# Where a second-layer operand is staged between two matrix products of a one-core kernel: out of the buffers of the weight jobs, into the places of the streamed weights

## The chip, the cores and the metric

The kernel runs on one core of a Trainium2 chip. The metric is the device time of one execution in microseconds. The engines are named as the profile names them: PE (TensorE, matrix products), DVE (VectorE), ACT (ScalarE), POOL (GpSimd), SP (SyncE, which only issues DMAs). Each engine runs its own instructions in order; DMAs are issued from the queues of SP, ACT and POOL.

## The reference

```
x  = attention(q, k, v)              # 8 x 8 heads, 576 x 64, masked with decay gamma^(i-j)
x  = x.reshape(4608, 512)
h  = (x @ w1) * (x @ w2)             # 512 -> 1024
x2 = (h @ w3) @ w_out                # 1024 -> 512; w3 @ w_out is multiplied out once
h2 = x2 @ w_in                       # 512 -> 2048
g  = h2 * clip(h2 + 3, 0, 6) / 6
out = g @ w_out2                     # 2048 -> 512, float32
```

## The kernel before

Every float32 operand is split into a high part (rounded on ACT) and a low part (a subtraction on DVE, `sub`, L134), and a product is three matmuls: high by high, high by low, low by high. The program is written as a sequence of ticks: one tick is three matmuls of 512 columns (`mm3`, L129 to L131, or seven matmuls per four ticks in the seven-product part), and `at(s, f)` puts f's instructions into the program at tick s. A tick sets only an order: each engine runs ahead of it or behind it as its waits allow. SP above all runs far ahead.

**Blocks.** After a prologue that multiplies w3 by w_out into W (high part `Wh`, low part `Wl`, `Wm`), the first layer runs over nine blocks j = 0 to 8 of 512 tokens. A block begins with `ffn1`: 16 products pa and pb (8 values f, for w1 and w2) in 64 ticks, four PSUM banks in turn. ACT copies pa out (`a_copy`, L642), DVE multiplies by pb (`s_mul`, L670 to L674), ACT rounds (`s_hi`, L681), DVE subtracts (`s_lo`, L134 with `pair`). Block 0 and block 8 have an older form (`ab_mul`, L657, `ab_hi`, L661). Between the products stand four "excursions" per block, the attention of a later block in small matmuls (L213); behind each, DVE has `v_scale` (L203), `z_sum` (L281), `p_mask` (L227), `s_add` (L246), `x_out` (L290) and `x_lo` (L134), ACT has `z_copy` (L274) and `x_hi` (L298).

**Seven products.** In blocks 1 to 7 the product of h with W is made of seven half-size products instead of eight (`px_str`, L769, 32 ticks). Its weights are sums of quarters of W, kept in the DRAM scratch `wsd` and streamed 1 MB at a time by SP (`load_w`, L726) into three places: two halves of the tile `wb`, and a third in the x tile of the block that has just been used (`w3`, tag `xl`). Product i + 3 is loaded into the place of product i. The first two loads of the next block are issued as soon as their places are free.

**x2.** The result of a block is x2, in the x tile with tag `xh` (`rt`). It is prepared for the second layer in two halves m = 0 and 1: four sums (`x2_sums`, DVE), high part (`x2_hi`, L812, ACT), low part (`x2_lo`, DVE), and two stores of 896 KB in 1 KB pieces to `xod` (`x2_store`, L822, from ACT's queue). This stands at ticks 1, 2, 3 and 7 behind the block for m = 0, and 14 ticks later for m = 1, so in the next block's ffn1. Sums and low part go to `stg`, the high part to `stg_hi`.

**Jobs.** `stg` and `stg_hi` also carry the weights of the second layer: per block a job i (w_in) and a job q (w_out2). A job loads two raw pieces on SP (`fetch`, L106), unpacks them into `stg` (`weights`: ACT L154, L155; DVE L159, L163) at ticks s to s + 5, has four sums (L838) at s + 10, the high part (ACT, L841) at s + 11, the low part at s + 14 and two stores (L849, ACT's queue) at s + 19. Job i stands at s = 30 of the block, job q at 58; in the last block at 24 and 50.

**The last block.** W is read back from `wsd` into the place of `wb` (`w_again`, L577 to L582, ten DMAs, 4 MB) from tick 2 of block 8 on. The first operands of the second layer (`load_xop`, L902, 1 MB each) come from tick 24 on. In block 0, `w_quads` (L565 to L570, ten DMAs, 4 MB) stores W's quarters at tick 20, and four `w_job`s make the other weights of the stream at ticks 65, 73, 81 and 97.

Of the kernel before, what the change touches and what calls it, by code (L numbers as in the profile page):

```python
# [26 lines left out]
def retention_moe_kernel(  # L27
# [57 lines left out]
    wsd = dram_p.tile([8, 128, 2, 4, 256], F32, name="wsd")  # L85
# [233 lines left out]
    with tc.manual_schedule():  # L319
# [152 lines left out]
        for t in range(2 * TPB, NTI):  # L472
            ex[t] = B0 + SPB * (t // TPB - 1) + 16 + 22 * (t % TPB)
# [83 lines left out]
        def open_sw():  # L557
            st["wb"] = Wp.tile([128, 2, 2, 4, 256], F32R, tag="Wh", name="wb")
# [50 lines left out]
        at(B0 + 20, w_quads)  # L609
        for q, d in enumerate((65, 73, 81, 97)):  # L610
# [5 lines left out]
        def ffn1(j):  # L616
# [29 lines left out]
            def f_b(f):  # L646
# [41 lines left out]
                for d, f_ in enumerate((s_mul, s_hi, s_lo) if j in STR else (ab_mul, ab_hi, ab_lo)):  # L688
# [664 lines left out]
```

## Time and profile before

| | us |
|---|---|
| time, median of 3 runs | 1558.53 (1558.18 to 1559.66) |
| the profiled execution | 1558.04 |
| its span, first to last instruction | 1556.2 |
| PE busy | 1453.1 (93% of the span) |
| DVE busy | 1111.3 (71%) |
| ACT busy | 587.1 (38%) |
| POOL busy | 139.9 (9%) |
| mean granted clock of PE | 0.979 of full speed |

An engine is busy while one of its instructions runs; issuing a DMA and waiting are not counted. The blocks j = 0 to 8 lie from 72.75 to 855.03 us of the span, the second layer from there to the end. A wait is read from the idle time ahead of an instruction, shown in brackets with what ended it. A granted clock below 1.00 in a stretch means that PE ran part of it at 1.2 instead of 2.4 GHz.

### The profile page before, as it was taken

The page shows a single profiled execution, that of the slowest core. Times are in us where ns is not written, and L with a number is a line of the kernel's source. Part 1 is how long each engine was busy: PE and PEld are TensorE (multiplying, and loading weights), DVE is VectorE, ACT ScalarE, POOL GpSimd, SP SyncE. Part 2 cuts the span into 40 slices and gives each one's busy share as a digit, 9 for nine tenths or more (in the row PEclk, how much of TensorE's full clock was granted, in tenths as well). Part 3 has the DMA queues.
Part 4 walks back from the last instruction along what each step waited for, and adds up shares of the span by engine and source line. Part 5 has one row for each costly group of instructions (what it writes and reads, how often), then busy time and mean ns, then how long its engine had stood idle before and what let it go on. Part 6 is the DMA issues. An engine that isn't in the chain of part 4 may idle for free.

```text
span 1556.2 us, 27873 instructions
## 1 busy us (share of the span) xinstructions
PE 1453.1 (93%) x11315; PEld 1219.0 (78%) x11315; DVE 1111.3 (71%) x1916; ACT 587.1 (38%) x878; POOL 139.9 (9%) x293
## 2 busy tenths in 40 slices
PE   9998898988988898887959999999999999999999
PEld 4577687776867777776848789888888888888888
DVE  7878576757568585767723766566667988888887
ACT  7563242323334242423412434333334434444443
POOL 1000000000000000000000124222222000000000
PEclk9999999999999999999989999999999999999999
DMA  9774667674857666684687987464688644444442
GB/s 353 264 243 149 231 231 264 236 282 174 317 173 271 220 239 255 213 293 165 236 323 300 337 305 257 177 242 169 259 312 315 192 136 136 136 137 136 133 140 75
DMA packets 195056, 351.30 MB, mean 226 GB/s; under 512 B 10384, under 2 KB 143280, under 8 KB 185072
## 3 DMA queue, kind: packets, MB, share of 16 engines
q1 hardware_dynamic: 122832, 212.88, 39.4%
q0 software_dynamic: 21792, 73.72, 12.8%
q10 hardware_dynamic: 50304, 62.92, 11.9%
q8 instruction: 89, 1.46, 0.4%
q14 instruction: 39, 0.32, 0.1%
HBM read 231.51 MB, written 117.96 MB: 225 GB/s over the span
## 4 chain that ended last, share of the span: by engine, by line
PE 52%; DMA 18%; DVE 17%; ACT 8%; issue 3%; SPq 1%; ACTq 0%; POOL 0%; DVEq 0%; POOLq 0%
PE pb L1275 15%; DMA xod<-stg 9%; DMA wqd<-stg 8%; PE pb L1276 8%; PE pb L129 8%; PE pb L131 8%; PE pb L130 8%; DVE stg L134 3%; PE Wps L512 3%; DVE x L290 2%; DVE stg L159 1%; ACT stg L154 1%; DVE stg L163 1%; ACT sign L155 1%; ACT pair L681 1%
## 5 line engine op out<-in xcount | busy, mean ns | idle before, releaser
L1275 PE MATMUL pb<-wq,op 128*128 128x512 f32 x1000 | 346.7, 391 | 0.0
L1276 PE MATMUL pb<-wq,op 128*128 128x256 f32 x1000 | 280.0, 280 | 0.0
L1275 PEld LDWEIGHTS pb<-wq,op 128*128 128x128 f32 x1000 | 187.0, 187 | 41.0
L129 PE MATMUL pb<-xop,wset 128*128 128x512 f32 (+1 forms) x558 | 205.6, 369 | 2.0 <-DMA xop<-xod 1.4
L130 PE MATMUL pb<-xop,wset 128*128 128x512 f32 (+1 forms) x558 | 205.2, 368 | 0.0
L131 PE MATMUL pb<-xop,wset 128*128 128x512 f32 (+1 forms) x558 | 205.2, 368 | 0.0
L1153 ACT CAST op<-unit 128x1024 fp32r<-128x1024 f32 x126 | 131.6, 1052 | 173.6 <-DVE unit L1139 152.8
L1276 PEld LDWEIGHTS pb<-wq,op 128*128 128x128 f32 x1000 | 189.0, 189 | 0.0
L134 DVE TENSOR_TENSOR op<-unit,op 128x1024 fp32r<-128x1024 f32 x126 | 153.9, 1222 | 30.6 <-ACT op L1153 30.6
L769 PE MATMUL px<-pair,wb 128*128 128x256 f32 x1176 | 154.3, 291 | 15.0 <-ACT pair L681 5.7
L769 PEld LDWEIGHTS px<-pair,wb 128*128 128x128 f32 x1176 | 148.2, 197 | 20.5 <-ACT pair L681 7.3
L129 PE MATMUL pb<-xh,w2h 128*128 128x512 f32 x288 | 120.2, 417 | 35.3 <-DVE sraw L674 12.8
L129 PE MATMUL pa<-xh,w1h 128*128 128x512 f32 x280 | 113.7, 406 | 28.0 <-ACT a L642 26.9
L129 PEld LDWEIGHTS pb<-xop,wset 128*128 128x128 f32 x558 | 105.2, 189 | 20.4 <-issue 1.8
L131 PEld LDWEIGHTS pb<-xop,wset 128*128 128x128 f32 x558 | 105.2, 189 | 17.5
L130 PEld LDWEIGHTS pb<-xop,wset 128*128 128x128 f32 x558 | 105.2, 189 | 17.3
L130 PE MATMUL pb<-xl,w2h 128*128 128x512 f32 x288 | 117.0, 406 | 0.0
L131 PE MATMUL pb<-xh,w2l 128*128 128x512 f32 x288 | 116.9, 406 | 0.0
L130 PE MATMUL pa<-xl,w1h 128*128 128x512 f32 x280 | 112.1, 400 | 0.2 <-DVE xl L134 0.2
L131 PE MATMUL pa<-xh,w1l 128*128 128x512 f32 x280 | 111.5, 398 | 0.0
L134 DVE TENSOR_TENSOR stg<-x 128x256 f32<-128x256 f32 x31 | 13.1, 422 | 125.7 <-DMA wqd<-stg 64.7
L129 PEld LDWEIGHTS pb<-xh,w2h 128*128 128x128 f32 x288 | 56.7, 197 | 53.5 <-issue 14.8
(200 smaller groups left out, 2330.1 us busy)
## 6 DMA issues: line engine op xcount, KB each, us to landing
wb<-wsd SPq DMA_DIRECT2D x49, 1024.0 KB, 5.7
unit<-gd SPq DMA_DIRECT2D x72, 512.0 KB, 5.3
xop<-xod SPq DMA_DIRECT2D x28, 1024.0 KB, 6.7
qk<-in_qk_dram POOLq DMA_DIRECT2D x36, 512.0 KB, 6.7
kv<-in_kv_dram POOLq DMA_DIRECT2D x32, 512.0 KB, 5.7
gd<-gw POOLq DMA_DIRECT2D x60, 256.0 KB, 2.9
gd<-g POOLq DMA_DIRECT2D x57, 256.0 KB, 3.8
xod<-stghi ACTq DMA_DIRECT2D x16, 896.0 KB, 4.7
```

The source lines that it names most:

```text
L129: nc.tensor.matmul(out=out_ap, lhsT=sh, rhs=mh, start=first, stop=False, **kw)
L130: nc.tensor.matmul(out=out_ap, lhsT=sh, rhs=ml, start=False, stop=False, **kw)
L131: nc.tensor.matmul(out=out_ap, lhsT=sl, rhs=mh, start=False, stop=last, **kw)
L134: eng.tensor_tensor(out=out_ap, in0=x, in1=y, op=ALU.subtract)
L154: nc.scalar.activation(out=c["u"], in_=high, func=ACTF.Abs, scale=2.0 ** -112)
L155: nc.scalar.activation(out=c["s"].bitcast(F16).rearrange("p (n t) -> p n t", t=2)[:, :, 1], in_=high, func=ACTF.Copy, scale=2.0 ** -64)
L290: nc.vector.scalar_tensor_tensor(out=c["x32"][:, p, a:a + n], in0=c["z"][:, p, a:a + n], scalar=cw[:, m, p:p + 1], in1=ut[:, p, 0:n], op0= ...
L512: nc.tensor.matmul(out=ps, lhsT=w3f[:, n // 4 % 8, n % 4 * 128:n % 4 * 128 + 128], rhs=wo[:, j, :], start=j == 0, stop=j == KF - 1)
L769: nc.tensor.matmul(out=out_ap, lhsT=w[:, x, kk, ms], rhs=y, start=k not in seen, stop=kk == 3 and x == 1, skip_group_check=True)
L1153: nc.scalar.copy(out=op_tiles(7 * b + p)[0], in_=src())
L1275: nc.tensor.matmul(out=c[k], lhsT=h[:, ts], rhs=w, start=first and kt == 0, stop=False, skip_group_check=True)
L1276: nc.tensor.matmul(out=c[k][:, 0:256], lhsT=l[:, ts], rhs=w[:, 0:256], start=False, stop=kt == 7, skip_group_check=True)
```

## The change

Six things change:

- x2 of blocks 1 to 7 no longer goes through `stg` and `stg_hi`. Its sums go to a new tile `xs` (the other x tile of the block, tag `xl`, which held the third streamed weight), one half of it for each m; its high and low parts go to the two halves of `wb`, the same for both m. Stores stand at tick 6 instead of 7, and m = 1 stands 16 ticks behind m = 0 instead of 14.
- `wsd` is laid out so that a streamed weight is read in pieces of 2 KB instead of 8 KB.
- `w_again` moves from tick 2 to tick 30 of block 8, and the memset of the sign tile (`late_sign`) from 0 to 23.
- `w_quads` moves from tick 20 to 44 of block 0, the last `w_job` from 97 to 104.
- Job i moves from tick 30 to 22, job q from 58 to 50 (in the last block from 50 to 48).
- The excursions of a block stand at 19, 40, 61 and 82 instead of 16, 38, 60 and 82, and `s_lo` one tick later.

```diff
-    wsd = dram_p.tile([8, 128, 2, 4, 256], F32, name="wsd")
+    wsd = dram_p.tile([8, 4, 128, 2, 256], F32, name="wsd")
...
-            ex[t] = B0 + SPB * (t // TPB - 1) + 16 + 22 * (t % TPB)
+            ex[t] = B0 + SPB * (t // TPB - 1) + 19 + 21 * (t % TPB)
...
-            st["wb"] = Wp.tile([128, 2, 2, 4, 256], F32R, tag="Wh", name="wb")
+            st["wb"] = Wp.tile([128, 2, 4, 2, 256], F32R, tag="Wh", name="wb")
...
-        at(B0 + 20, w_quads)
-        for q, d in enumerate((65, 73, 81, 97)):
+        at(B0 + 44, w_quads)
+        for q, d in enumerate((65, 73, 81, 104)):
...
-                for d, f_ in enumerate((s_mul, s_hi, s_lo) if j in STR else (ab_mul, ab_hi, ab_lo)):
+                for d, f_ in zip((0, 1, 3), (s_mul, s_hi, s_lo)) if j in STR else enumerate((ab_mul, ab_hi, ab_lo)):
...
-            nc.sync.dma_start(out=t.rearrange("p h k n -> p (h k n)").bitcast(F32), in_=wsd[WORD[i]].rearrange("p h k n -> p (h k n)"))
+            nc.sync.dma_start(out=t.rearrange("p k h n -> p k (h n)").bitcast(F32), in_=wsd[WORD[i]].rearrange("k p h n -> p k (h n)"))
...
-            for m, s in enumerate((now[0], now[0] + 14)):
-                def start(m=m):
-                    raw2.update({0: rt[:, m], 1: rt[:, 2 + m]})
-                    x2b["hi"], x2b["lo"] = stg_hi, stg
-                    x2_sums()
-
-                for d, f in ((1, start), (2, x2_hi), (3, x2_lo), (7, lambda m=m: x2_store(j, m))):
-                    at(s + d, f)
+            xs = x_ps[e].tile([128, 2, 4, 256], F32, tag="xl", name="xs")
+            hl = [st["wb"][:, i].rearrange("p k h n -> p (k h) n") for i in range(2)]
+            for m, s in enumerate((now[0], now[0] + 16)):
+                b1, b2, d = rt[:, m], rt[:, 2 + m], xs[:, m]
...
+                def sums(d=d, v=(b11, b12, b21, b22)):
+                    for o, a, b in ((0, v[1], v[0]), (1, v[3], d[:, 0]), (2, v[3], v[1]), (3, v[2], d[:, 1])):
+                        sub(nc.vector, d[:, o], a, b)
+
+                def hi(parts_=parts_):
+                    for a, b, t in parts_:
+                        nc.scalar.copy(out=hl[0][:, a:b], in_=t)
+
+                def lo(parts_=parts_):
+                    for a, b, t in parts_:
+                        sub(nc.vector, hl[1][:, a:b], t, hl[0][:, a:b])
+
+                def store(m=m):
...
+                    for h, t in enumerate(hl):
+                        nc.scalar.dma_start(out=xod[sb][:, :, m, h, a:a + HB1].rearrange("o p n -> p o n"), in_=t[:, 0:7].bitcast(F32))
+
+                for x, f in ((1, sums), (2, hi), (3, lo), (6, store)):
+                    at(s + x, f)
...
-            job(("i", n), (w_in2[n + NSET], w_in2[n]), A_SUMS, lambda hl, n=n: wid[n, hl], B0 + SPB * n + SPB + (30 if n < NSET - 1 else 24))
+            job(("i", n), (w_in2[n + NSET], w_in2[n]), A_SUMS, lambda hl, n=n: wid[n, hl], B0 + SPB * n + SPB + (22 if n < NSET - 1 else 24))
...
-                lambda hl, n=n: wqd[:, :, n, hl].rearrange("o p n -> p o n"), B0 + SPB * n + SPB + (58 if n < NSET - 1 else 50))
+                lambda hl, n=n: wqd[:, :, n, hl].rearrange("o p n -> p o n"), B0 + SPB * n + SPB + (50 if n < NSET - 1 else 48))
...
...
-        at(E0, late_sign)
+        at(E0 + 23, late_sign)
-        for i, s in enumerate((24, 52, 26, 28, 32, 38, 104)):
+        for i, s in enumerate((24, 58, 26, 28, 32, 38, 104)):
...
-        at(B0 + SPB * (STR[-1] + 1) + 2, w_again)
+        at(B0 + SPB * (STR[-1] + 1) + 30, w_again)
```

The first place in which the order of instructions matters is DVE at the start of a block (here block 6): the last sum of the seven products, then x2 of m = 0. Before, everything is written to `stg`, which a job's store may still be reading:

```order
L744 TENSOR_TENSOR x_5635<-x_5635,px 128x2x256 x2
L134 TENSOR_TENSOR stg<-x_5635 128x256
L134 TENSOR_TENSOR stg<-x_5635,stg 128x256
L134 TENSOR_TENSOR stg<-x_5635 128x256
L134 TENSOR_TENSOR stg<-x_5635,stg 128x256
L134 TENSOR_TENSOR stg<-x_5635,stghi 128x512
L134 TENSOR_TENSOR stg<-x_5635,stghi 128x256
L134 TENSOR_TENSOR stg<-stg,stghi 128x1024
```

The same instructions of DVE in the changed kernel, at the same place:

```order
L746 TENSOR_TENSOR x_5643<-x_5643,px 128x2x256 x2
L134 TENSOR_TENSOR xs<-x_5643 128x256
L134 TENSOR_TENSOR xs<-x_5643,xs 128x256
L134 TENSOR_TENSOR xs<-x_5643 128x256
L134 TENSOR_TENSOR xs<-x_5643,xs 128x256
L134 TENSOR_TENSOR wb<-x_5643,wb 128x512
L134 TENSOR_TENSOR wb<-x_5643,wb 128x256
L134 TENSOR_TENSOR wb<-xs,wb 128x1024
```

Their number and their sizes are the same; what they write to is another place.

The second place is DVE at the end of ffn1 (block 5), where the seven products are about to begin: `zp`, `P`, `S`, `x` and `xl` are an excursion's work, `stg` a job's, `keep` and `sraw` the `s_mul` of f = 7, and `pair` its `s_lo`, on which the third product waits. Before:

```order
L134 TENSOR_TENSOR xl<-x_5611,xh 128x4x128
L159 SCALAR_TENSOR_TENSOR stg<-stg,sign 128x512
L163 SCALAR_TENSOR_TENSOR stg<-wr,stg 128x512
L673 TENSOR_TENSOR keep<-a,pb 128x256
L674 TENSOR_TENSOR sraw<-a,pb 128x256
L134 TENSOR_TENSOR sraw<-keep,sraw 128x256 x2
L134 TENSOR_TENSOR keep<-sraw 128x256
L134 TENSOR_TENSOR pair<-sraw,pair 128x768
L838 TENSOR_TENSOR stg<-stg 128x256 x4
L134 TENSOR_TENSOR stg<-stg,stghi 128x1792
```

DVE at the same place of the changed kernel:

```order
L859 TENSOR_TENSOR stg<-stg 128x256 x4
L281 TENSOR_TENSOR zp<-zp,z 128x512
L227 TENSOR_TENSOR P<-sc,mask 128x512
L244 COPY S<-sc 128x256
L246 TENSOR_TENSOR S<-S,sc 128x256
L290 SCALAR_TENSOR_TENSOR x_5627<-zp,cw,ut 128x128 x4
L134 TENSOR_TENSOR xl<-x_5627,xh 128x4x128
L134 TENSOR_TENSOR stg<-stg,stghi 128x1792
L675 TENSOR_TENSOR keep<-a,pb 128x256
L676 TENSOR_TENSOR sraw<-a,pb 128x256
L134 TENSOR_TENSOR sraw<-keep,sraw 128x256 x2
L134 TENSOR_TENSOR keep<-sraw 128x256
```

The job's four sums and its 1792-column subtraction have moved from behind the last `pair` row to ahead of it, and the last unpacking (L159, L163) out of this stretch. The `pair` row is the next one.

The third place is SP in block 8: the end of `w_again` (`Wh`, `Wl`, `Wm`), the raw pieces of the last jobs (`wr`) and the operands of the second layer (`xop`). Before:

```order
L582 DMA Wl<-wsd 128x4x256
L577 DMA Wh<-wsd 128x4x256
L579 DMA Wl<-wsd 128x256
L580 DMA Wm<-wsd 128x3x256
L106 DMA wr<-in_w_in_dram 128x512 x2
L902 DMA xop<-xod_66 128x2048 x4
L106 DMA wr<-in_w_out_dram 128x512
```

SP in the changed kernel, from the same DMA of `w_again` on:

```order
L584 DMA Wl<-wsd 128x4x256
L579 DMA Wh<-wsd 128x4x256
L581 DMA Wl<-wsd 128x256
L582 DMA Wm<-wsd 128x3x256
L923 DMA xop<-xod_66 128x2048
L106 DMA wr<-in_w_out_dram 128x512
L923 DMA xop<-xod_66 128x2048
L106 DMA wr<-in_w_out_dram 128x512
```

The raw pieces of job i and three of the `xop` loads now stand ahead of `w_again`, and the raw pieces of job q right behind it.

## Rows read from the trace of the kernel before

**Rows 1.** Windows, span and busy: blocks 2 to 7; ffn1; seven products; block 8

```profile
core 0: us, PE busy (x) PEld busy (x) DVE busy (x) ACT busy (x) POOL busy (x), PEclk, DMA share, GB/s
244.94:771.01 526.07, 462.88 (x4994) 394.33 (x4993) 353.24 (x704) 176.65 (x276) 28.56 (x45) 0.96 0.66 236
331.06:391.90 60.84, 52.97 (x546) 42.51 (x545) 37.88 (x75) 19.88 (x32) 3.82 (x6) 0.97 0.58 204
655.88:681.46 25.58, 23.10 (x281) 22.18 (x280) 21.05 (x45) 8.95 (x14) 1.27 (x2) 1.00 0.89 322
771.01:833.27 62.26, 46.43 (x194) 37.54 (x193) 25.20 (x41) 17.39 (x28) 0.59 (x8) 0.89 0.77 276
```

**Rows 2.** Waits of PE, blocks 2 to 7: us in total, times, longest

```profile
PE pa L129 <- ACT a L642: 13.7, 6, 3.1
PE pb L129 <- DVE sraw L674: 12.8, 5, 4.1
PE sc L213 <- DVE kv L203: 12.1, 12, 1.8
```

**Rows 3.** Waits of DVE, blocks 2 to 7, in the same columns

```profile
DVE stg L134 <- DMA wqd<-stg: 49.9, 6, 9.0
DVE stg L134 <- DMA xod<-stg: 38.5, 6, 8.4
```

**Rows 4.** Timeline of DVE, block 3: start, duration, instruction, [idle before]

```profile
340.07 0.43 DVE L134 TENSOR_TENSOR stg<-x 128x256 f32<-128x256 f32 x1 [8.12 <-DMA wqd<-stg]
...
388.29 0.68 DVE L670 TENSOR_TENSOR sraw<-a,pb 128x512 f32<-128x512 f32 x1
...
397.50 0.69 DVE L159 SCALAR_TENSOR_TENSOR stg<-stg,sign 128x512 int32<-128x512 int32 x1 [0.58 <-ACT sign L155]
...
401.15 0.96 DVE L134 TENSOR_TENSOR pair<-sraw,pair 128x768 fp32r<-128x768 f32 x1 [0.56 <-ACT pair L681]
402.03 1.55 DVE L838 TENSOR_TENSOR stg<-stg 128x256 f32<-128x256 f32 x4
405.33 2.03 DVE L134 TENSOR_TENSOR stg<-stg,stghi 128x1792 fp32r<-128x1792 f32 x1 [1.75 <-ACT stghi L841]
```

**Rows 5.** Timeline of PE, the seven products of block 3

```profile
401.17 0.38 PE L769 MATMUL px<-pair,wb 128*128 128x256 f32 x1 [1.20 <-ACT pair L681]
402.16 5.22 PE L769 MATMUL px<-pair,wb 128*128 128x256 f32 x29 [0.61 <-DVE pair L134]
```

**Rows 6.** DMA from 392 to 403, weights alone: packets, MB, share; issues

```profile
q1 hardware_dynamic: 432, 3.15, 77.0%
...
wb<-wsd SPq DMA_DIRECT2D x3, 1024.0 KB, 4.8
```

**Rows 7.** DMA from 360 to 368, stores of x2 alone

```profile
q10 hardware_dynamic: 1824, 1.84, 69.3%
...
xod<-stg ACTq DMA_DIRECT2D x1, 896.0 KB, 6.3
```

**Rows 8.** DMA issues from 403 to 430, all three queues: KB, us to landing

```profile
wb<-wsd SPq DMA_DIRECT2D x4, 1024.0 KB, 8.4
...
wqd<-stg ACTq DMA_DIRECT2D x1, 896.0 KB, 20.6
```

**Rows 9.** Timeline of PE, block 0

```profile
109.50 0.77 PE L129 MATMUL pb<-xh,w2h 128*128 128x512 f32 x1 [3.50 <-DVE ab L657]
...
129.74 0.57 PE L213 MATMUL sc<-kv 64*64 64x64 f32 x15 [4.62 <-DVE kv L203]
```

**Rows 10.** Timeline of ACT, block 0

```profile
105.98 0.66 ACT L154 ACTIVATE stg<-wr 128x512 f32<-128x512 f32 x1 [9.91 <-DMA wr<-in_w_dram]
```

**Rows 11.** Timeline of ACT, block 8

```profile
811.03 0.66 ACT L154 ACTIVATE stg<-wr 128x512 f32<-128x512 f32 x1 [16.75 <-DMA xod<-stg]
```

**Rows 12.** Timeline of PE, block 8

```profile
814.53 0.80 PE L129 MATMUL pa<-xh,w1h 128*128 128x512 f32 x1 [13.23 <-ACT a L642]
```

**Rows 13.** DMA from 88 to 105: 1 KB stores of W

```profile
DMA packets 4663, 5.69 MB, mean 335 GB/s; under 512 B 203, under 2 KB 4299, under 8 KB 4661
```

More of the change, by code (lines that the diff above doesn't have):

```diff
@@ L576, in w_again @@
             for o, (c, k) in enumerate(quads):
-                nc.sync.dma_start(out=h[:, k:k + 4, c:c + 256].bitcast(F32), in_=wsd[o, :, 0])
+                src = wsd[o].rearrange("k p h n -> p h k n")
+                nc.sync.dma_start(out=h[:, k:k + 4, c:c + 256].bitcast(F32), in_=src[:, 0])
                 if k:
-                    nc.sync.dma_start(out=lo[0][:, 4:5, c:c + 256].bitcast(F32), in_=wsd[o, :, 1, 0:1])
-                    nc.sync.dma_start(out=lo[1][:, :, c:c + 256].bitcast(F32), in_=wsd[o, :, 1, 1:4])
+                    nc.sync.dma_start(out=lo[0][:, 4:5, c:c + 256].bitcast(F32), in_=src[:, 1, 0:1])
+                    nc.sync.dma_start(out=lo[1][:, :, c:c + 256].bitcast(F32), in_=src[:, 1, 1:4])
                 else:
-                    nc.sync.dma_start(out=lo[0][:, 0:4, c:c + 256].bitcast(F32), in_=wsd[o, :, 1])
+                    nc.sync.dma_start(out=lo[0][:, 0:4, c:c + 256].bitcast(F32), in_=src[:, 1])
         def w_job(q, s):
@@ L603, in store @@
                 for hl, t in enumerate((st["w"][1], st["w"][0])):
-                    nc.scalar.dma_start(out=wsd[4:8, :, hl, q].rearrange("o p n -> p o n"), in_=t[:, 1].rearrange("p (o n) -> p o n", o=4))
+                    nc.scalar.dma_start(out=wsd[4:8, q, :, hl].rearrange("o p n -> p o n"), in_=t[:, 1].rearrange("p (o n) -> p o n", o=4))
             for d, f in ((0, sums), (2, hi), (3, lo), (6, store)):
                 at(s + d, f)
-        at(B0 + 20, w_quads)
-        for q, d in enumerate((65, 73, 81, 97)):
+        at(B0 + 44, w_quads)
+        for q, d in enumerate((65, 73, 81, 104)):
             w_job(q, B0 + d)
@@ L730, in px_str @@
             rt = x_ps[e].tile([128, 4, BLK1], F32, tag="xh", name="x1")
-            st["w3"] = x_ps[e].tile([128, 2, 4, 256], F32R, tag="xl", name="wb")
+            st["w3"] = x_ps[e].tile([128, 4, 2, 256], F32R, tag="xl", name="wb")
             a, c, b, d = turn
@@ L768, in px_str @@
                         for x, y in ((0, hi), (0, lo), (1, hi)):
-                            nc.tensor.matmul(out=out_ap, lhsT=w[:, x, kk, ms], rhs=y, start=k not in seen, stop=kk == 3 and x == 1, skip_group_check=True)
+                            nc.tensor.matmul(out=out_ap, lhsT=w[:, kk, x, ms], rhs=y, start=k not in seen, stop=kk == 3 and x == 1, skip_group_check=True)
                             seen.add(k)
```

13 lines of the change are left out of this document (9 added, 4 removed).

## The prediction

> **What bounds the kernel now.** I read the windows first. Blocks 2 to 7 take 526.07 us, 87.7 each; PE is busy for 462.88 of them, so it stands idle for 63.2 us (10.5 a block), and the granted clock is 0.96, which is 4% of 87.7 = 3.5 us a block lost to stretches at 1.2 GHz [rows 1]. Nothing else is near full: DVE is busy for 353.24 us, 58.9 a block. So PE bounds these blocks, with holes, and the question is who makes the holes. PE's own waits name DVE and ACT: 13.7 us for `a_copy`, 12.8 for the `s_mul` of a large f, 12.1 for `v_scale` [rows 2]. DVE's waits say why it was late: 49.9 us for the store of job q and 38.5 for x2's own store of m = 0, together 88.4 us or 14.7 a block, all ahead of x2's sums [rows 3]. Block 3 shows the pattern: the sums of m = 0 wait 8.12 us at 340.07, because job q's low part still leaves `stg` [rows 4]. That store takes 20.6 us from issue to landing, where a store of the same size takes 6.3 behind its twin with nothing else in flight [rows 7, 8]. DVE takes its instructions in order, so `s_mul` and `v_scale` stand behind the blocked sums, PSUM banks stay full, and PE stops. Behind a stop the clock drops.
>
> **x2 out of `stg`.** No instruction is added. Before, x2's sums waited for job q and for x2's first store, and job i's unpacking for x2's second store. Now the sums write `xs`, which no DMA reads, so both waits of DVE [rows 3] lose their reason. What replaces them: the high and low parts of m = 1 go to the same halves of `wb` as those of m = 0 and must wait for the stores of m = 0. These are issued at tick 6, m = 1's high part stands at tick 18. Twelve ticks are 12 x 0.68 = 8.2 us, where a tick is 51.2 us of ffn1 without its three excursions (7.7 us), divided by 64. A store alone lands in 6.3 us [rows 7], and the queue is then empty of job q, which is issued 8 ticks earlier. I take no wait here; if the stores land as late as 10 us, 2 us a block. Behind the waiting instruction ACT has `s_hi` and `z_copy`, and PE has 12 ticks before it misses a bank, so even that is mostly covered.
>
> What is late next is DVE's own queue. Without the blocked 14.7 us it has 58.9 us of work a block plus its pauses for ACT, against PE's 74.3 (below). In ffn1 the load is dense, and the end of ffn1 gets more: ahead of the last `pair` row there now stand job q's sums and low part. Before, from the `s_mul` of f = 3 (388.29) to the end of `s_hi` of f = 7 (401.1) was 12.8 us [rows 4]. Out go two unpackings of 2 x 0.69 with their 0.6 us waits for ACT, 3.9 us. In come the sums 1.55, ACT's high part that now stands ahead of `z_copy` and costs DVE 1.75, and the low part 2.03 [rows 4]: 5.3 us. So 14.2 us. PE needed that row at 401.17 - 1.20 = 399.97 [rows 5]. If DVE starts the stretch as late as before, PE waits 1.2 + 1.4 = 2.6 and then 0.6 for `s_lo`, 3.2 us; if it is 2 us later, because PE itself no longer waits for it in ffn1, 5.2. I take 4.3, against 1.8 before. `s_lo` one tick later lets other work into DVE's pauses for `s_hi`, such as the 0.56 us at 401.15 [rows 4]; I count nothing for it.
>
> **A block now.** PE alone: ffn1 52.97 us busy at clock 0.97, less 3% of 60.84, is 51.1; the seven products at clock 1.00 are 23.10 [rows 1]; 74.2. To this come 4.3 for the pair, 0.9 for `v_scale` (2.0 before, 12.1 / 6; the half that came from blocked DVE goes), 0.5 for a weight that is late, and 1.7 for the clock (half of 3.5, one drop behind the pair wait). Sum 81.6, against 87.7: 6.1 us a block, 36.6 over the six. As a check, 74.2 + 10.5 + 3.5 = 88.2 gives the block before within 0.5.
>
> **2 KB pieces.** A load of 8 KB pieces moves 3.15 MB in 77.0% of 16 engines x 11 us, 23.2 GB/s per engine; stores in 1 KB pieces 1.84 MB in 69.3% of 16 x 8 us, 20.7 [rows 6, 7]. 2 KB lies between, so a 1 MB load occupies its engines for 2.8 to 3.2 us, at most 0.3 more, and lands after some 5 us alone. The gap that matters is contention: with all queues busy a load takes 8.4 us and a 1 KB store 20.6 [rows 8], as if the queues took turns by piece. Then smaller pieces shorten the store and lengthen the load. The slack of a load is two products, 6 us, plus the pair wait; job q's stores are issued 8 ticks earlier and overlap loads that are wanted later. I keep 0.5 us a block, with 0 and 3 as ends. The Trainium skill, DMA: Bandwidth & Descriptors, section Queues, rings and completion order, says that each DMA engine takes turns between its queues by packet; the two latencies above agree in direction. By it a load of 32 pieces per engine gives way to at most 32 pieces of 1 KB, which at 20.7 GB/s are 1.6 us; that lies between the ends above.
>
> **The first two loads of a block** now wait for x2's second store, since their places hold x2. Job q's raw pieces stand behind them on SP, and ACT and DVE wait for those. By ticks: m = 1's stores leave at about 21 us of the block (DVE some 4 us behind tick 22), land at 27, both loads at 33, the raw pieces at 35; job q wants them at tick 50, 39 us. Cost nothing; that cover is 4 us thick.
>
> **Blocks 0 and 1.** `w_quads` moved behind the last raw pieces on SP. Before, ACT waited 9.91 us for a raw piece queued behind those ten DMAs [rows 10]; DVE went idle, and PE lost 3.50 and then 4.62 us to its backlog [rows 9]. SP runs ahead of ticks, so `w_quads` really moves by some 5 us only, which is enough. Gain 8, between 3 and 10. Job 0 now comes 8 ticks earlier, onto a store of block 0 that still uses `stg`: +1 (0 to 3). Together -7.
>
> **Block 8.** PE waited 13.23 us for `a_copy`, behind ACT's 16.75 for x2's store [rows 11, 12]. That goes. But `w_again` (4.2 MB) now starts when x2's last store has landed, and job q's raw pieces stand behind it on SP. From tick 22 (15 us) to the second raw piece move: x2's stores 1.8 MB, four `xop` 4.2, `w_again` 4.2, job i's stores 1.8, a fifth `xop` 1.0, raw pieces 1.0: 14.1 MB at 335 GB/s [rows 13] is 42 us, so 57 us of the block. ACT stands in front of `a_copy` of f = 6 until then, and PE, which without a wait is through ffn1 at 64 x 0.68 = 43.5, waits some 14 us. One wait takes the place of the other: 0, from -8 to +8.
>
> **Sum.** 1558.0 (the profiled execution) - 36.6 - 7 + 0 = 1514.4; the median of the runs is 0.5 above it: **1515 us**. The second layer is untouched.
>
> **Rivals.**
> - No lag at all. DVE has 58.9 us for 74 us of PE's. If it reaches the last pair in time, a block is 74.2 + 0.5 + 0.9 = 75.6, 12.1 saved, 72.6 in all: 1478. For it: `v_scale` and `s_lo` have ticks to spare. Against: DVE's order at the end of ffn1.
> - DVE becomes the bound. Its work and its remaining pauses for ACT come in ffn1 to about as much as PE's 51, so a backlog past 8 us there would stop PE at the banks again: half of the 26.5 us of the first two waits [rows 2] stays (2.2 a block), with the clock's 1.7: 85.5 a block, 13 saved, and with block 0 1538.
> - Late weights, slower. If x2's second store takes the 16 us that ACT waited for one in block 8 [rows 11] instead of 6, the two loads land at 45, the raw pieces at 50, ACT stands 11 us at job q, 8 of it covered; PE loses 3 and the last pair comes 8 later (12 instead of 4.3): 74.2 + 12 + 3 + 0.9 + 0.5 + 3.5 = 94.1, +6.4 a block, and +8 in block 8: 1558 + 38 + 8 - 7 = 1597. It decides once that store lands after some 31 us of the block. Against: the queues are emptier than before at that time.
> - Nothing gained: PE's holes move from ffn1 into the pair wait in full (10 us), a block stays at 87.7, and what block 0 gains is waited out in block 1: 1558.
>
> **Numbers.** Forecast 0.55, no lag 0.15, DVE the bound 0.18, late weights 0.08, nothing gained 0.04. The forecast's own spread is the pair wait (3.2 to 5.2), late weights (0 to 3) and block 8: 1495 to 1535. Range 1478 to 1541: it takes in the second and third case and leaves out the last two. A change of 0.2% (3 us) is about what can be told from none. Faster 0.88, same 0.04, slower 0.08.
>
> **What would show it.** Right: DVE's waits for `wqd<-stg` and `xod<-stg` gone from blocks 2 to 7; ffn1 near 52 us, with no wait for `a` or `sraw` over 1 us; the seven products longer, near 28, with 3 to 5 us in front of the third; in block 0 no 9.91 us wait of ACT; in block 8 ACT's long wait now for `wr<-in_w_out`. Wrong: `xs` or `wb` rows of DVE or ACT waiting for `xod`; PE waiting for `wb<-wsd` by more than 1 us a block; ffn1 still at 60.

## The result, and the profile after

The changed kernel takes 1537.22 us (median of 3, 1534.01 to 1537.32), 0.9855 of the time before, 95% interval [0.9833, 0.9877]: 21 us faster. The forecast was 1515, its range 1478 to 1541. The profiled execution took 1534.01 us, its span 1532.2.

Where the time went, from the first and last product of each stretch in the two traces (us):

| stretch | before | after | moved | forecast |
|---|---|---|---|---|
| block 0 | 87.6 | 79.9 | -7.7 | -8 |
| block 1 | 84.6 | 92.4 | +7.8 | +1 |
| blocks 2 to 7 | 526.1 | 503.4 | -22.7 | -36.6 |
| block 8 | 84.0 | 81.7 | -2.4 | 0 |
| second layer | 701.2 | 702.0 | +0.8 | 0 |

Windows of the kernel after: blocks 2 to 7, then ffn1 and the seven products of block 3, block 1, ffn1 of block 8. The columns are those of [rows 1].

```profile
core 0: us, PE busy (x) PEld busy (x) DVE busy (x) ACT busy (x) POOL busy (x), PEclk, DMA share, GB/s
245.13:748.53 503.40, 459.42 (x4995) 400.25 (x4993) 354.49 (x704) 178.63 (x276) 28.02 (x44) 0.95 0.71 247
327.27:380.62 53.35, 50.30 (x547) 41.53 (x546) 39.42 (x77) 20.51 (x32) 3.82 (x6) 1.00 0.63 223
380.62:411.54 30.92, 25.54 (x297) 24.85 (x296) 19.65 (x39) 9.27 (x15) 1.27 (x2) 0.89 0.84 298
152.71:245.13 92.42, 80.32 (x856) 68.10 (x857) 59.74 (x117) 30.21 (x47) 5.09 (x8) 0.93 0.73 251
748.53:806.95 58.42, 43.71 (x195) 35.86 (x193) 23.68 (x39) 17.17 (x27) 0.69 (x6) 0.91 0.78 274
```

PE's waits in blocks 2 to 7 of the kernel after (us in total, times, longest), against [rows 2]: the waits for `a_copy` and for the large `s_mul` are gone, so no PSUM bank is late in ffn1. In their place the third product waits for its `pair` (25.3 us in both rows, 4.2 a block), and the attention waits longer for `v_scale` (16.7 against 12.1).

```profile
PE px L771 <- ACT pair L683: 22.4, 6, 5.0
PE sc L213 <- DVE kv L203: 16.7, 6, 3.8
PE px L771 <- DVE pair L134: 2.9, 6, 0.6
PE px L771 <- DMA wb<-wsd: 1.8, 2, 1.3
```

DVE's waits there, against [rows 3]: the 88.4 us for `wqd<-stg` and `xod<-stg` are gone. DVE's longest waits for another engine than PE are now for ACT's half of a job's unpacking (before: 26.1 us in 24 waits, the longest 3.3).

```profile
DVE stg L159 <- ACT sign L155: 35.7, 18, 4.3
DVE zp L281 <- ACT zp L274: 15.3, 12, 2.2
```

The end of ffn1 in block 3 shows both waits grow. The lines are of ACT, DVE and PE, each in order of time:

```profile
373.48 0.69 ACT L154 ACTIVATE stg<-wr 128x512 f32<-128x512 f32 x1 [1.88 <-DMA wid<-stg]
...
383.03 1.69 ACT L862 CAST stghi<-stg 128x1792 fp32r<-128x1792 f32 x1 [1.74 <-DVE stg L859]
384.62 0.58 ACT L274 COPY zp<-z 128x512 f32<-128x512 f32 x1
```

```profile
374.87 0.69 DVE L159 SCALAR_TENSOR_TENSOR stg<-stg,sign 128x512 int32<-128x512 int32 x1 [3.81 <-ACT sign L155]
...
377.07 0.68 DVE L203 TENSOR_TENSOR kv<-kv,rate 128x512 f32<-128x512 f32 x1
...
385.23 0.42 DVE L281 TENSOR_TENSOR zp<-zp,z 128x256 f32<-128x256 f32 x1 [2.24 <-ACT zp L274]
...
389.38 2.02 DVE L134 TENSOR_TENSOR stg<-stg,stghi 128x1792 fp32r<-128x1792 f32 x1
...
393.63 0.96 DVE L134 TENSOR_TENSOR pair<-sraw,pair 128x768 fp32r<-128x768 f32 x1 [0.56 <-ACT pair L683]
```

```profile
377.81 0.69 PE L213 MATMUL sc<-kv 64*64 64x64 f32 x32 [3.05 <-DVE kv L203]
...
393.65 0.58 PE L771 MATMUL px<-pair,wb 128*128 128x256 f32 x1 [4.96 <-ACT pair L683]
394.65 1.65 PE L771 MATMUL px<-pair,wb 128*128 128x256 f32 x6 [0.41 <-DVE pair L134]
```

Read from the first line down: job q's first unpacking waits on ACT until job i's store has left `stg` (373.4), DVE waits for ACT (374.87), `v_scale` is behind that (377.07), and PE stands for 3.05 us at 377.81. Then job q's sums, ACT's high part in front of `z_copy` and the low part (389.38) stand ahead of the last `pair`; PE waits for that at 393.65. The store is part of PE's wait, not all of it: ACT waits for it in blocks 3 to 7 (9.4 us together), and in block 2, where ACT does not wait for it, PE still stands 1.30 us for `v_scale`, because job q's first unpacking stands right ahead of `v_scale` on DVE. Job i's store lands late when other transfers are in flight with it (below, the run with both jobs back shows it without them). All DMA of the kernel after from 359 to 374, the packets and MB of ACT's queue, and the issues (KB, us to landing):

```profile
DMA packets 1521, 5.23 MB, mean 348 GB/s; under 512 B 128, under 2 KB 128, under 8 KB 1520
...
q10 hardware_dynamic: 288, 1.84, 29.1%
...
wid<-stghi ACTq DMA_DIRECT2D x1, 896.0 KB, 10.5
wid<-stg ACTq DMA_DIRECT2D x1, 896.0 KB, 10.1
kv<-in_kv_dram POOLq DMA_DIRECT2D x1, 512.0 KB, 10.2
qk<-in_qk_dram POOLq DMA_DIRECT2D x1, 512.0 KB, 14.0
```

Job i's two stores go in pieces of 7 KB (1.84 MB in 288 packets), unlike x2's, which go in 1 KB pieces (1.84 MB in 1824 packets, [rows 7]). The same two stores in block 3 of the kernel before, 377 to 392, had the engines nearly to themselves:

```profile
wid<-stghi ACTq DMA_DIRECT2D x1, 896.0 KB, 3.6
wid<-stg ACTq DMA_DIRECT2D x1, 896.0 KB, 3.8
```

In block 8 of the kernel after, ACT's long wait has the new name that was foretold, and PE stands 14.71 us behind it (13.23 before, [rows 11, 12]):

```profile
801.43 0.66 ACT L154 ACTIVATE stg<-wr 128x512 f32<-128x512 f32 x1 [15.79 <-DMA wr<-in_w_out_dram]
...
806.95 0.79 PE L129 MATMUL px<-abh,Wh 128*128 128x512 f32 x1 [14.71 <-ACT a L644]
```

### The profile page after: what moved, and what is told of

It is laid out like the page before. It is cut to its first block, busy times and chain, and to the rows that moved or that the text cites. A ratio compares the mean times of both kernels' runs of the same rounds, so it can differ in the third digit from the quotient of the medians.

```text
span 1532.2 us, 27909 instructions
## 1 busy us (share of the span) xinstructions
PE 1449.1 (95%) x11315; PEld 1224.6 (80%) x11315; DVE 1113.2 (73%) x1916; ACT 588.7 (38%) x878; POOL 139.5 (9%) x293
## 4 chain that ended last, share of the span: by engine, by line
PE 60%; DVE 19%; DMA 10%; ACT 8%; issue 3%; SPq 0%; ACTq 0%; POOL 0%; DVEq 0%; POOLq 0%
PE pb L1296 15%; PE pb L129 8%; PE pb L1297 8%; PE pb L131 8%; PE pb L130 8%; PE px L771 6%; DMA wid<-stg 3%; PE Wps L512 3%; DVE stg L134 2%; ACT stghi L862 2%; DVE pair L134 2%; DVE stg L159 2%; DVE stg L163 1%; DVE x L290 1%; DVE stg L859 1%
## 5 line engine op out<-in xcount | busy, mean ns | idle before, releaser
L771 PE MATMUL px<-pair,wb 128*128 128x256 f32 x1176 | 164.5, 303 | 33.0 <-ACT pair L683 27.7
L771 PEld LDWEIGHTS px<-pair,wb 128*128 128x128 f32 x1176 | 159.0, 210 | 38.7 <-ACT pair L683 29.1
L129 PE MATMUL pb<-xh,w2h 128*128 128x512 f32 x288 | 116.3, 404 | 3.2 <-DVE sraw L672 2.9
L683 ACT CAST pair<-sraw 128x512 fp32r<-128x512 f32 (+1 forms) x56 | 40.7, 727 | 154.7 <-DVE sraw L134 154.7
L1160 DVE TENSOR_TENSOR unit<-unit 128x1024 f32<-128x1024 f32 x72 | 87.9, 1220 | 0.6
```

Source lines behind the costliest of these rows:

```text
L129: nc.tensor.matmul(out=out_ap, lhsT=sh, rhs=mh, start=first, stop=False, **kw)
L683: nc.scalar.copy(out=st["pair"][f % 4][:, 0, a:b], in_=st["raw"][:, a + 1:b + 1])
L771: nc.tensor.matmul(out=out_ap, lhsT=w[:, kk, x, ms], rhs=y, start=k not in seen, stop=kk == 3 and x == 1, skip_group_check=True)
L1160: nc.vector.tensor_tensor(out=f32_unit(o), in0=t[0], in1=t[1], op=f)
```

## The experiments

Theory A: x2's new place brings the gain, and the jobs' new ticks give much of it back, by job q's part ahead of the last `pair` and by its unpacking behind job i's slow store. All ratios are to runs of the kernel before on the same chip (its medians there: 1558.59 us for the first four kernels behind "after" in the table, 1560.45 for the next four, 1560.72 for the last four). The times of blocks come from the one profiled execution of each kernel, which can lie some us off its median: 5.1 above it with both jobs back, 3.9 below it with x2's place alone.

| kernel | us | ratio [95%] | blocks 0, 1, 2 to 7, 8 (us) |
|---|---|---|---|
| before | 1558.5 | | 87.6, 84.6, 526.1, 84.0 |
| after | 1537.2 | 0.9855 [0.9833, 0.9877] | 79.9, 92.4, 503.4, 81.7 |
| both jobs back | 1498.0 | 0.9609 [0.9584, 0.9635] | 79.4, 84.7, 481.6, 80.4 |
| jobs alone | 1542.9 | 0.9896 [0.9879, 0.9914] | 87.5, 93.1, 500.3, 83.3 |
| job q back | 1496.6 | 0.9589 [0.9566, 0.9613] | 79.7, 87.9, 470.3, 81.4 |
| late operands | 1525.1 | 0.9780 [0.9763, 0.9797] | 79.4, 92.1, 506.4, 68.0 |
| 8 KB pieces | 1528.8 | 0.9795 [0.9772, 0.9818] | 79.4, 93.3, 498.8, 81.5 |
| q back, late operands | 1482.7 | 0.9495 [0.9467, 0.9523] | 79.6, 85.5, 472.1, 68.0 |
| the same, 8 KB | 1464.7 | 0.9385 [0.9361, 0.9409] | 79.6, 84.6, 450.4, 72.4 |
| q at 68, late operands | 1458.0 | 0.9341 [0.9320, 0.9362] | 79.3, 85.6, 445.6, 67.6 |
| the same, 8 KB | 1458.0 | 0.9350 [0.9324, 0.9376] | 79.4, 83.7, 446.4, 72.7 |
| the same, last weight job at 97 | 1463.3 | 0.9385 [0.9351, 0.9419] | 79.6, 84.8, 444.9, 72.9 |
| x2's place alone | 1487.8 | 0.9536 [0.9509, 0.9562] | 87.8, 82.4, 454.9, 80.8 |
| quarters' store back | 1544.6 | 0.9902 [0.9874, 0.9930] | 87.3, 91.9, 508.9, 81.8 |

**Both jobs back to their ticks.**

```diff
-  ... B0 + SPB * n + SPB + (22 if n < NSET - 1 else 24))
+  ... B0 + SPB * n + SPB + (30 if n < NSET - 1 else 24))
-  ... B0 + SPB * n + SPB + (50 if n < NSET - 1 else 48))
+  ... B0 + SPB * n + SPB + (58 if n < NSET - 1 else 50))
```

> The changed kernel with the jobs where they stood before: job i at tick 30, job q at 58 (24 and 50 in the last block). Theory A (x2's place brings the gain, the jobs' new ticks give part of it back): the wait for the third product's pair goes from 4.2 us a block to near 1.8, the wait of the attention for v_scale from 2.8 to about 1, one clock drop of some 3 us a block goes, so 3 to 5 us a block less in blocks 1 to 7: 1502 to 1516. Rival B (DVE's total work is the bound at the end of ffn1, wherever the jobs stand): the waits only change name, 1533 to 1541. Rival C (the earlier jobs are needed, because job q's store would again be late for something): slower than the changed kernel, above 1541.

1498.0 us: 39 us faster than the changed kernel, 4 below theory A's range. Rivals B and C fall. Blocks 2 to 7 lost both waits (1.9 us are left for the `pair`, none for `v_scale`), block 1 its 7.8 us. A new wait appeared, 28.0 us for streamed weights; the first row of PE's waits in blocks 2 to 7:

```profile
PE px L771 <- DMA wb<-wsd: 28.0, 12, 4.2
```

**The jobs alone, on the kernel before.**

```diff
-  ... (30 if n < NSET - 1 else 24))
+  ... (22 if n < NSET - 1 else 24))
-  ... (58 if n < NSET - 1 else 50))
+  ... (50 if n < NSET - 1 else 48))
```

> The kernel before with nothing changed but the jobs' ticks (i at 22, q at 50; 48 in the last block). Theory A (the gain is x2's place): x2's sums still write the buffer that the jobs' stores read. Job q's store leaves 8 ticks (5 us) earlier, so DVE's wait for it falls from 8.3 a block to 3 or 4, but job i now stands one tick behind x2's second store in the same buffer and must wait for it 4 us or more, and the pair waits 2 us longer: within 10 us of the kernel before, 1548 to 1568. Rival C (the jobs' ticks are a large part of the gain): 1545 or less.

1542.9 us, 16 faster than before: theory A's number failed, rival C's held. DVE's wait for job q's store did not fall to 3 or 4 us a block; it went altogether, and that for x2's store halved. ACT has the wait that was expected for job i. Waits of DVE and ACT in blocks 2 to 7 of this kernel, against [rows 3]:

```profile
DVE stg L134 <- DMA xod<-stg: 18.9, 6, 4.1
...
ACT stg L154 <- DMA xod<-stg: 34.9, 6, 5.9
```

So moving the jobs and moving x2 are two cures for the same stall, the jobs' a partial one: it leaves these two waits for x2's stores, and 12.4 us of PE's waits for `s_mul`. With the jobs early, blocks 2 to 7 take 500.3 us with x2 in `stg` and 498.8 (8 KB pieces) with x2 out of it: x2's place adds next to nothing there.

**Job q alone back, job i stays early.**

```diff
-  ... B0 + SPB * n + SPB + (50 if n < NSET - 1 else 48))
+  ... B0 + SPB * n + SPB + (58 if n < NSET - 1 else 48))
```

> The changed kernel with job q alone put back to tick 58 in blocks 1 to 7; job i stays at 22. Theory A: both losses come from job q: its unpacking stands in ffn1 behind job i's store (landing late, 10 us), and its sums stand ahead of the last pair. With q at 58 both are gone, though job i's store is as slow as now: 1502 to 1518, within 5 us of the run with both jobs put back. Rival D (it is job i's early place, whose store collides with the loads): no more than a third of what the run with both jobs back gains.

1496.6 us, 1.4 from the run with both back; rival D falls. Job i's store is as slow as in the changed kernel, but nobody waits for it: in blocks 2 to 7 its second half lands in 8.7 to 10.4 us, against 3.5 to 4.8 with both jobs back, so it is job i's early place that makes it slow. PE's waits in blocks 2 to 7 of this kernel, and DMA issues in block 3 from 350 to 365:

```profile
PE px L771 <- DMA wb<-wsd: 18.9, 11, 3.3
...
PE sc L213 <- DVE kv L203: 1.1, 3, 0.6
PE px L771 <- DVE pair L134: 0.6, 1, 0.6
```

```profile
wid<-stghi ACTq DMA_DIRECT2D x1, 896.0 KB, 11.0
wid<-stg ACTq DMA_DIRECT2D x1, 896.0 KB, 10.4
```

Pair wait and `v_scale` wait, 42 us in the changed kernel, are 1.7 here: both come from job q's tick. How much each of the two waits is worth alone was not tried. What is left is the weights.

**x2's place alone** (the changed kernel with 8 KB pieces, both jobs back as above, and these lines back; the excursions' ticks stay).

```diff
-        at(B0 + 44, w_quads)
-        for q, d in enumerate((65, 73, 81, 104)):
+        at(B0 + 20, w_quads)
+        for q, d in enumerate((65, 73, 81, 97)):
...
-  zip((0, 1, 3), (s_mul, s_hi, s_lo)) if j in STR else enumerate((ab_mul, ab_hi, ab_lo))
+  enumerate((s_mul, s_hi, s_lo)) if j in STR else enumerate((ab_mul, ab_hi, ab_lo))
```

> The changed kernel with all but x2's new place put back: 8 KB pieces, the jobs at 30 and 58 (24 and 50), the store of W's quarters at 20, the last weight job at 97, the high and low part of a large f one tick apart; what stays beside x2's place is what it needs (the weights read back later, one operand load later) and the excursions' ticks. Theory A (the place alone brings more than the whole change): 1498 (jobs put back) + 8 (block 0) - 15 (the last weight no longer late) - 3 (last weight job) = 1488, within 8. Rival L (the place needs some of the other edits, the distance of one tick above all): above 1505.

1487.8 us, where the sum said 1488: 71 us under the 1558.5 of the kernel before (73 under its own chip's 1560.7), more than three times what the whole change brings. DVE waits for no store in blocks 2 to 7. The sum hit the time and not each term: blocks 2 to 7 take 26.7 us less than with both jobs back, of which the wait for weights is the 15 that were summed and the rest is mostly clock (0.97 there, 1.00 here); and the two kernels lie 19.2 us apart by their profiled executions, 10.2 by their medians. Blocks 2 to 7 take 75.8 us each, and no wait for a `pair` or for `v_scale` is left (the window, then PE's largest wait):

```profile
242.95:697.82 454.87, 438.72 (x4994) 383.37 (x4993) 354.27 (x704) 178.58 (x277) 28.03 (x44) 1.00 0.76 276
```

```profile
PE px L771 <- DMA wb<-wsd: 13.0, 10, 2.2
```

With 8 KB pieces the four corners for blocks 2 to 7 are: 526.1 before, 500.3 jobs alone, 454.9 x2 alone, 498.8 both. The jobs' move is worth -26 us with x2 in `stg` and +44 with x2 out of it (the two runs with x2 out of it have the excursions' new ticks too, and the last one the new tick of `s_lo` and block 0's moves). It is job q's tick that costs the 44: the kernel with job q back, late operands and 8 KB pieces has the new tick of `s_lo` and job i's early place too, and takes 450.4 there. What the excursions' ticks bring by themselves was not tried.

**8 KB pieces in the changed kernel** (`wsd` and the tile `wb` in the layout before).

```diff
-    wsd = dram_p.tile([8, 4, 128, 2, 256], F32, name="wsd")
+    wsd = dram_p.tile([8, 128, 2, 4, 256], F32, name="wsd")
```

> The changed kernel with the streamed weights laid out in 8 KB pieces as before, nothing else. Theory A: smaller pieces let the 1 KB stores through and delay the loads; in the changed kernel nothing waits for job q's store any more and the loads have 5 us of slack behind the pair wait, but job i's store (10 us, for which the attention's v_scale already waits) would land later still: 1535 to 1547. Rival G (the pieces' size sets nothing here): 1534 to 1540. Rival H (larger pieces load faster, and that shortens something): below 1533.

1528.8 us: faster than with 2 KB (the intervals don't touch; 8.4 us by the medians, 3.7 by the two profiled executions), so rival H, and theory A's reason failed: job i's store lands as before in 10.2 us, not later. It is not a store in 1 KB pieces in the first place, as its packets above show. In blocks 2 to 7 PE waits 2.6 us less for `v_scale` and 0.6 less for the pair's high part than in the rows of the changed kernel, and the window is 4.6 us shorter; what made these two waits shorter was not settled.

```profile
PE px L771 <- ACT pair L683: 21.8, 6, 4.8
PE sc L213 <- DVE kv L203: 14.1, 6, 3.6
```

**Four operand loads of block 8 moved behind the weights read back and the last raw pieces.**

```diff
-        for i, s in enumerate((24, 58, 26, 28, 32, 38, 104)):
+        for i, s in enumerate((44, 58, 46, 48, 50, 52, 104)):
```

> The changed kernel with four loads of the second layer's first operands in block 8 (4 MB) moved behind the weights that are read back and the last job's raw pieces. Theory A (PE's 14.7 us wait in block 8 is the time that 14 MB need ahead of the last raw piece): 4 MB less at 335 GB/s are 12 us, so the wait falls to 2 to 6 us and the time to 1523 to 1531, if the second layer still finds its operands. Rival E (the queue's order is not what sets it, x2's last store or the weights' own transfer is): wait and time unchanged, 1533 to 1541. Rival F: the second layer waits for its operands in turn, 1537 or more.

1525.1 us; PE's wait in block 8 fell from 14.71 to 2.42, the second layer took 3.5 us more (705.5). Theory A had the number and the place; rivals E and F fall, though the 3.5 us are in F's direction. ACT's wait in block 8 of this kernel, and PE's behind it:

```profile
792.96 0.66 ACT L154 ACTIVATE stg<-wr 128x512 f32<-128x512 f32 x1 [11.84 <-DMA wr<-in_w_out_dram]
```

```profile
796.46 0.50 PE L129 MATMUL px<-abh,Wh 128*128 128x512 f32 x1 [2.42 <-ACT a L644]
```

**Job q back and the late operand loads together.**

> Job q back at tick 58 and the four late operand loads together. The two losses lie in different places (end of ffn1 in blocks 1 to 7; block 8), so by theory A the gains add: 1496.6 - 12.1 = 1484.5, within 5. If they share a cause (the DMA queues carried over from block 7 into block 8), they don't add: 1490 or more.

1482.7 us: the gains add, each in its place (blocks 2 to 7 take 472.1 us, block 8 68.0).

**The same with 8 KB pieces.**

> The same with 8 KB pieces. With job q at 58, the seven products wait for their last weight in every block (18.9 us over blocks 2 to 7 with the clock drops behind it), which takes 11.8 us from issue to landing because job q's two stores and the next job's raw pieces are in flight beside it. Theory A (the queues take turns by piece): 8 KB pieces give the load a larger share, the wait for the weight goes (as in the kernel before, where it was under 1 us), job q's store lands in 20 us instead of 16, which nobody waits for: 3 to 5 us a block faster than with 2 KB, 1460 to 1472. Rival G (the engines are full, 333 GB/s, whatever the piece): within 4 us of the run with 2 KB. Rival I (job q's store so late that x2's stores or job i's unpacking wait): slower than with 2 KB.

1464.7 us, as theory A said, and the clock is at 1.00 in blocks 2 to 7. The issues of one burst at the end of block 3's seven products, first with 2 KB (381.8 to 386), then with 8 KB (374.6 to 379):

```profile
wb<-wsd SPq DMA_DIRECT2D x1, 1024.0 KB, 11.9
...
wqd<-stghi ACTq DMA_DIRECT2D x1, 896.0 KB, 16.1
wqd<-stg ACTq DMA_DIRECT2D x1, 896.0 KB, 16.6
```

```profile
wb<-wsd SPq DMA_DIRECT2D x1, 1024.0 KB, 8.9
...
wqd<-stghi ACTq DMA_DIRECT2D x1, 896.0 KB, 15.0
wqd<-stg ACTq DMA_DIRECT2D x1, 896.0 KB, 15.5
```

With larger pieces the weight lands 3.0 us sooner here, and the stores beside it land no later (my 20 us for them was wrong). Over blocks 2 to 6 the last load takes 11.3 us in the mean with 2 KB and 8.9 with 8 KB; job q's two stores take 12.6 and 15.8 with 2 KB, 13.6 and 15.4 with 8 KB. The Trainium skill, DMA: Bandwidth & Descriptors, section Queues, rings and completion order, says that a DMA engine takes turns between queues by packet; the load's 3.0 us agree with it in direction, if a load in fewer, larger pieces needs fewer turns. The turns themselves are not shown: in the first 8 us behind the issue of job q's first store, SP's queue moved 1.84 MB and ACT's 0.95 with 2 KB pieces, 1.90 and 0.92 with 8 KB (means of the same blocks), so neither queue got a clearly larger share. That larger pieces bring the load in sooner is shown; by what mechanism is open.

**Job q at 68, 2 KB pieces, late operand loads.**

```diff
-  ... (58 if n < NSET - 1 else 48))
+  ... (68 if n < NSET - 1 else 48))
```

> 2 KB pieces, the four late operand loads, and job q at tick 68 instead of 58, so that its stores leave at tick 87, behind the seven products' last load, and the next job's raw pieces come later too. Theory A (the last weight is late because job q's stores and the raw pieces are in flight with it): the wait for it falls from 3 us to under 1.5, but job q's unpacking, sums and low part now stand among the seven products and delay DVE there; 1468 to 1484. Rival J (DVE's work in the seven products, 20.8 of 30 us busy, becomes what PE waits for): 1485 or more.

1458.0 us, better than expected; rival J falls, DVE has room among the seven products. Its stores now leave behind the last load, and PE's waits in blocks 2 to 7 are down to 9 us, most of it in the first row below (its window first):

```profile
237.43:683.01 445.58, 436.72 (x4994) 381.67 (x4993) 353.75 (x704) 177.28 (x276) 28.04 (x44) 1.00 0.80 281
```

```profile
PE px L771 <- DMA wb<-wsd: 6.8, 7, 1.4
PE px L771 <- issue: 1.1, 1, 1.1
```

A block takes 74.3 us. This is the fastest version found, 6.6% under the kernel before; the next one equals it.

**The same with 8 KB pieces.**

> The version with job q at 68 and the late operand loads, with 8 KB pieces. With q at 68 its stores leave behind the last load, so the load has little beside it: the 6.8 us that PE still waits for weights over blocks 2 to 7 shrink to 2 to 4, 1450 to 1458. If the pieces' size matters only where a store is in flight with the load, the same as with 2 KB, within 3.

1458.0 us: no difference in time. PE's waits for weights did fall, from 6.8 to 3.5 us, as the first theory said, but other short waits came instead (9.6 us of waits in all, 8.8 with 2 KB). For the kernel's time the size of the pieces matters where a store is in flight with the load, and not once the store has been moved away. (In the versions with 8 KB and late operands block 8 took 4 to 5 us more than with 2 KB, 72.4 and 72.7 here against 68.0 and 67.6; why, was not looked into.)

**The quarters' store and the last weight job back in block 0.**

```diff
-        at(B0 + 44, w_quads)
-        for q, d in enumerate((65, 73, 81, 104)):
+        at(B0 + 20, w_quads)
+        for q, d in enumerate((65, 73, 81, 97)):
```

> The changed kernel with the store of W's quarters back at tick 20 of block 0 and the last of the four weight jobs back at 97. Theory A (block 0's 7.7 us came from this move alone): ACT waits some 10 us for a raw piece again and block 0 goes from 79.9 to about 87.6; in block 1, DVE's wait for ACT behind the last weight job's store (PE's gap of 2.94 and a clock drop) goes: 3 to 4 back; 1537.2 + 7.7 - 3.5 = 1541, 1537 to 1546. Rival K (block 0 gained from the excursions' new ticks): block 0 stays at 80, time 1534 or less.

1544.6 us. Block 0 is back at 87.3 and ACT waits for its raw piece again, against [rows 10]; rival K falls. The part on block 1 failed: it stays at 91.9, since PE's gap only goes to another place there, where ACT waits for x2's store of block 0. Two lines of ACT in this kernel:

```profile
105.43 0.66 ACT L154 ACTIVATE stg<-wr 128x512 f32<-128x512 f32 x1 [9.58 <-DMA wr<-in_w_dram]
...
172.74 0.59 ACT L819 COPY stg<-px 128x512 f32<-128x512 f32 x1 [9.48 <-DMA xod<-stg]
```

**The last weight job alone back, in the best version with 8 KB pieces.**

```diff
-        for q, d in enumerate((65, 73, 81, 104)):
+        for q, d in enumerate((65, 73, 81, 97)):
```

> The same with the last of the four weight jobs back at tick 97 of block 0 (the store of W's quarters stays at 44). Theory A: ACT's 5.2 us wait for that job's store in block 1 goes, and with it PE's gap of 2.6 us and a clock drop of 3.4 us at half speed: 3 to 4 us less than with 104. Rival M: the job's raw piece is then late, behind the quarters' store, and block 0 pays it: the same or slower.

1463.3 us, no gain (the intervals of the two overlap). Theory A fell here, and rival M's mechanism too, as block 0 is unchanged (79.6). Again the wait of block 1 moved: PE's 2.85 us gap behind the job's store is gone, and one of 4.52 us stands behind x2's store of block 0. ACT in this kernel:

```profile
166.71 0.58 ACT L819 COPY stg<-px 128x512 f32<-128x512 f32 x1 [10.73 <-DMA xod<-stg]
```

## Why the prediction was right, and where it was wrong

The direction was right, the size too large: 21 us instead of 43. The signs named for it appeared (DVE's waits for stores gone, ffn1 at 53.35 us in block 3, the wait in front of the third product, the new name of ACT's wait in block 8); the seven products took 30.92 us there instead of near 28, and no sign asked what the new waits in ffn1 would cost. By its own steps:

- **x2 out of `stg`: right.** Both waits of DVE and the bank waits of PE are gone. `xs` and `wb` rows wait for no store. Alone, the place brings 71 us, which is close to the rival without lag: its 75.6 us a block against 75.8 measured with x2's place alone. This is agreement in the sum and not in its terms: PE is busy for 73.1 of them instead of 74.2, weights cost 2.2 instead of 0.5, and `v_scale` nothing instead of 0.9. That rival's condition ("if DVE reaches the last pair in time") is what the jobs' move prevented.
- **The pair wait: right.** 4.3 forecast, 4.2 measured; from the `s_mul` of f = 3 (379.01) to the end of the high part of f = 7 (392.77 + 0.83) are 14.6 us, against 14.2 in the working. By block it is 2.7 to 5.4, least in block 7, where `v_scale` cost most (3.79) and PE came to the pair later; so the mean owes something to the wait that the next step left out. I booked it as a cost of the change as a whole. It is the jobs' alone (24.6 us with the jobs alone on the kernel before), and avoidable: 0.1 a block with job q back.
- **`v_scale`, 0.9: wrong, 2.8 measured (16.7 / 6).** The step that failed is the paragraph on the first two loads of a block. It counted x2's stores, the two loads and the raw pieces, and found a cover of 4 us. It left out job i's own two stores and the loads of k, v, q, which the same move puts into the same stretch. The loads, raw pieces, stores and these are 2.1 + 1.0 + 1.8 + 1.0 = 5.9 MB, at the 348 GB/s of that stretch 17 us; job i's second store took 10.1 us to land instead of 3.8, and job q's unpacking, as near behind job i as before, waited for it. In block 3 the step's times hold as far as the first load (x2's last store gone at 20.9 us of the block, landed at 27.8, the load at 33.2); then the second load lands at 37.1, the second raw piece at 45.6 instead of 35 and job i's second store at 46.1, with ACT at job q's unpacking from 44.3. ACT's wait for that store is 9.4 us, 1.6 a block, and 1.2 of the 2.8 are left without it, near the 0.9 of the forecast.
- **The clock, 1.7: wrong, 4.2 measured** (0.95 of 83.9). I counted one drop a block, behind the pair wait. In blocks 4 to 7 the `v_scale` wait brings a second, and of the pair's six drops four last 6.8 us at 1.2 GHz, where nine of the ten drops of the kernel before lasted 3.4.
- **A late weight, 0.5:** 0.3 measured. The step gave smaller pieces 0 to 3 us a block as their price. Measured are 0.8 in the changed kernel (503.4 - 498.8), inside it, and 3.6 with job q back and late operands (472.1 - 450.4), above it. In the changed kernel the price shows mostly in waits that are not for weights. The 1.6 us from turns take one turn to be one piece on either side, which no run shows.
- **PE alone, 74.2:** 503.4 / 6 less the waits (7.3) and the clock (4.2) leaves 72.4, 1.8 under it; the best version's whole block is 74.3. This term was too high and hid part of what the waits and the clock had too low. Together: 81.6 - 1.8 + 1.9 + 2.5 - 0.1 - 0.2 = 83.9.
- **Block 0, -8: right**, with its cause.
- **Block 1, +1: wrong, +7.8.** I priced only job 0's meeting with a store of block 0. But block 1 has the same jobs and the same seven products as blocks 2 to 7, so it pays the pair wait and the `v_scale` wait (8.6 us together, 1.2 before), and its granted clock falls from 0.96 to 0.93. It has nothing to gain, as block 0's x2 still goes through `stg`: DVE waits 9.6 us for it, 10.5 before. With the jobs put back, block 1 is at 84.7; with the jobs alone on the kernel before, at 93.1.
- **Block 8, 0: right.** 14 us foretold for the new wait, 14.71 measured (the second raw piece is unpacked 56.6 us into the block, 57 foretold), and the run that takes 4 MB from ahead of the raw piece confirms the sum of bytes.
- **The rivals.** "DVE becomes the bound" gave 1538, near the measured time, but for another reason: half of the waits at the banks was to stay, and none did. The late weights didn't come: x2's stores land in some 4 to 7 us in blocks 2 to 7.

Against the forecast for the profiled execution (1514.4, measured 1534.0) blocks 2 to 7 make up 13.9 us, 2.3 a block, and block 1 6.8; blocks 0 and 8 and the second layer together give 1.3 back. The other 2.7 us to the median are the profiled execution, which was 3.2 us under it this time and not 0.5.

## What to carry to other kernels

When a change holds two cures for one stall, price each with the other in place: here either one removed most of the wait in blocks 2 to 7, and the jobs' move on top of x2's then only cost its own side effects. When work is moved in time, list everything that it issues and all that is in flight at the new time, and add the bytes; and apply the per-stage costs to the stages that don't share the gain too. A short wait in front of PE can cost more than its length, by the clock behind it: in blocks 2 to 7 of the changed kernel, ten of the twelve waits for `v_scale` and for the pair were followed by 3.4 or 6.8 us at 1.2 GHz.

## What was not expected of the hardware

- The size of a piece decides how a load fares beside stores: 1 MB in 2 KB pieces landed in 11.9 us, in 8 KB pieces in 8.9, and the stores beside it landed at about the same time. With the stores moved away, the whole kernel took 1458.0 us with either.
- An 896 KB store in 1 KB pieces took 6.3 us to land in [rows 7], 15.0 to 16.6 in the rows above and 20.6 in [rows 8], by what else was in flight. Job i's, in 7 KB pieces, took 3.6 to 11.0; with job q at 58 in both kernels, issuing job i's second store 8 ticks earlier made it take 8.7 to 10.4 us instead of 3.5 to 4.8.
- With the waits gone, PE's clock stayed at 1.00 through blocks 2 to 7 (445.58 us), where 0.95 and 0.96 stood before: of the 58 us between the changed kernel and the best one there, 23 are clock, read from PE's busy time for the same matmuls (459.42 against 436.72), and the other 35 are waits.
